# Four column groups instead of two for the last eight rows of wo in a decode layer

## The chip, the cores and the metric

The kernel runs on one core of one Trainium2 chip. The metric is the device time of one execution in microseconds (us), as the median of several runs.

## The reference

One decode step of a layer with two parallel branches, added to the residual x (1 x 1024), all operands bf16:

```
xn  = layernorm(x)
A   = softmax(q k^T / sqrt(128)) v @ wo      # q = xn @ wq: 32 heads of 128, 4 kv heads, last 4096 positions
B   = gelu(layernorm(xn) @ w1 + b1) @ w2 + b2   # w1: 1024 x 3584, w2: 3584 x 1024
out = x + A + B                              # 1 x 1024, wo: 4096 x 1024
```

The keys and values used are 4 x 4096 x 128 each. Together with the four weight matrices some 40 MB are read from memory for one row of output.

## The kernel before

The kernel is written with a tile library: the order of instructions on each engine is the order of the code, save that two places (`tc.issue_after`) tie a few instructions behind a named one, and the library adds the semaphore waits.

All large operands come in on one DMA queue, issued by SyncE in this order: the keys (`kq`), two halves of wq, w1, the values (`v_sb`), w2, and then wo. Each matrix goes into a tile of a small pool; a tile is loaded again when its last reader is done. wo (4096 rows of 1024) is laid out as 32 "rows" of 128 partitions x 1024 columns. Its first 16 rows come in one DMA, the second 16 rows in four: rows 0 to 7, 8 to 12, 13 and 14, and 15 of that half (`cuts` in L218).

The output of both branches is one sum over 60 such rows: 28 of w2, with columns of the hidden vector `hT` as weights, and 32 of wo, with columns of the attention output `o8` as weights. Every row is a contraction over 128 partitions with a single weight column, so the matmul writes one partition. The sum's 1024 columns are two halves of 512; each half has a column group of TensorE and a partition of its own (0 and 32), chosen with `tile_position=(0, 32 * half)`, so that the two halves' matmuls can run side by side. The first 52 rows are summed in the PSUM tile `accf` (L324), which also holds x and b2 from an earlier matmul (L179).

The last 8 rows, those of the last three DMAs, are summed apart (`TAIL = 8`). They go into two PSUM tiles `acct`, which split each half at column `N1 = 280`: `acct[0]` has columns 0 to 279, `acct[1]` columns 280 to 511. Both are first set to zero over 33 partitions by fp32 matmuls with zeros (L322), in the pause after the w2 rows. When `accf` is complete, ScalarE copies its columns 280 to 511 into `bulk[1]` (L328), and VectorE its columns 0 to 279 into `bulk[0]` (L329). Two fp32 matmuls of 33 rows with a column of the identity then bring `bulk[1]` into `acct[1]` (L333). Each tail row is four matmuls (L337): 280 columns for each half, then 232 columns for each half. At the end VectorE adds `acct[0]` and `bulk[0]` into the result row (L341), ScalarE copies `acct[1]` (L342), and two DMAs of one row of 512 values each write the output, one issued by SyncE (L344), one by ScalarE (L345).

At the start GpSimd fills constants: `zb` (with the bf16 identity and the selection matrices), `ones_f`, `mhalf`, `zf` (fp32 zeros and the selection matrix `sel4`) and `gmask`. `ident_f` is the fp32 identity.

Of the kernel before, what the change touches and what calls it, by code (L numbers as in the profile page):

```python
# [7 lines left out]
FP32 = mybir.dt.float32  # L8
BF16 = mybir.dt.bfloat16
ACT = mybir.ActivationFunctionType  # L10
ALU = mybir.AluOpType
# [4 lines left out]
def kernel(  # L16
# [14 lines left out]
    nc = tc.nc  # L31
    P = 128
# [5 lines left out]
    Hq = NQ // Dh  # L38
# [8 lines left out]
    CWO = NQ // P  # L47
# [5 lines left out]
    consts = ctx.enter_context(tc.tile_pool(name="consts", bufs=1))  # L53
# [5 lines left out]
    ps_f = ctx.enter_context(tc.tile_pool(name="ps_f", bufs=2, space=bass.MemoryType.PSUM))  # L59
# [3 lines left out]
    def ring_tile(name):  # L63
        return ring.tile([P, RING_ELEMS], BF16, tag="ring", name=name, align_bytes=256)
# [17 lines left out]
    for i in range(2):  # L82
        t = kq[:, RING_ELEMS:] if i == 0 else ring_tile("wq1")[:]
# [10 lines left out]
                            pattern=[[-1, P]], channel_multiplier=1)  # L94
    ident_f = consts.tile([P, P], FP32)
# [11 lines left out]
    with tc.issue_after(first_exp.ins):  # L107
# [1 line left out]
        nc.scalar.dma_start(out=xb8[0:4, :], in_=x_flat.rearrange("(a n) -> a n", a=4))  # L109
        nc.scalar.dma_start(out=xb8[4:8, :], in_=B_b2.rearrange("(a n) -> a n", a=4))  # L110
        nc.scalar.dma_start(out=b1_8[0:4, :], in_=b1_v[0:4, :])
    zf = consts.tile([P, 512 + Hq], FP32)
    nc.gpsimd.memset(zf[:], 0.0)
    zeros = zf[:, 0:512]
    sel4 = zf[:, 512:]
    qm_f = zb[:, P:P + 160]
    spread = zb[0:Hq, 288:800].rearrange("h (q p) -> h q p", q=4)
    sel_b = zb[0:8, 800:1056].rearrange("k (s m) -> k s m", s=2)
# [1 line left out]
    for sel, base in ((sel_x, 0), (sel_x, -64), (sel_b, 0)):  # L120
        nc.gpsimd.affine_select(out=sel, in_=sel, compare_op=ALU.not_equal, fill=1.0, base=base,
                                pattern=[[-16, 2], [-1, sel.shape[2]]], channel_multiplier=16)
    for R in range(4):
        nc.gpsimd.affine_select(out=sel4, in_=sel4, compare_op=ALU.not_equal, fill=1.0, base=-32 * R,
                                pattern=[[-1, Hq]], channel_multiplier=1)
# [3 lines left out]
                            pattern=[[-1, 4], [1, P]], channel_multiplier=-4)  # L129
# [4 lines left out]
                            pattern=[[-REP, Hkv]], channel_multiplier=1)  # L134
    nc.gpsimd.affine_select(out=gmask[:], in_=gmask[:], compare_op=ALU.is_ge, fill=0.0, base=REP - 1,
                            pattern=[[REP, Hkv]], channel_multiplier=-1)
# [35 lines left out]
    accf = ps_acc.tile([P, 512], FP32, tag="accf")  # L172
# [45 lines left out]
    for i, cuts in enumerate([[0, 16], [0, 8, 13, 15, 16]]):  # L218
        nr = CWO // 2
        t = ring_tile(f"wo{i}")  # L220
# [6 lines left out]
    for i, w3 in enumerate(wq_tiles):  # L227
        for r in range(4):
            c = 4 * i + r
            for j in range(NJQ):  # L230
                b, t = divmod(j, 4)
                nc.tensor.matmul(accq[32 * t:32 * t + 1, b, :], lhsT=xnT[:, c:c + 1], rhs=w3[:, r, j * 512:(j + 1) * 512],  # L232
                                 start=(c == 0), stop=(c == C - 1), tile_position=(0, 32 * t))
# [6 lines left out]
    for c in range(C):  # L240
        for b in range(2):
            for t in range(4):
                j = 2 * t + b
                nc.tensor.matmul(acch[32 * t:32 * t + 1, b, :NH], lhsT=yT[:, c:c + 1], rhs=w1v[:, c, j * NH:(j + 1) * NH],  # L244
                                 start=False, stop=(c == C - 1), tile_position=(0, 32 * t))
# [11 lines left out]
    for a in range(WQ4 // 512):  # L257
        for R in range(4):
            for g in range(Hkv):
                c0 = WQ4 * R + 512 * a  # L260
                nc.tensor.matmul(sp[32 * R:32 * R + 32, a, :], lhsT=qm[:, g, :], rhs=kT[:, g, c0:c0 + 512],  # L261
                                 start=(g == 0), stop=(g == Hkv - 1), tile_position=(0, 32 * R))
# [28 lines left out]
    hT = w2t[:, CW2 * D:CW2 * (D + 32)].rearrange("p (c f) -> p c f", f=32)  # L291
# [4 lines left out]
    for c in range(NCH):  # L296
        nc.tensor.matmul(o_all[:].rearrange("h g d -> h (g d)"), lhsT=eTb[:, 32 * c:32 * c + 32], rhs=v4[:, :, c, :],  # L297
                         start=(c == 0), stop=(c == NCH - 1))
# [6 lines left out]
    o8_ps = ps_f.tile([P, 32], FP32, tag="pf", name="o8_ps")  # L305
    for q in range(4):
        nc.tensor.matmul(o8_ps[:], lhsT=spread[:, q, :], rhs=o_bf[:, 32 * q:32 * q + 32], start=(q == 0), stop=(q == 3))
    o8 = consts.tile([P, 32], BF16)
    nc.scalar.copy(out=o8[:], in_=o8_ps[:])


    vec = {"h": lambda c: hT[:, c, 0:1], "o": lambda c: o8[:, c:c + 1]}
    N1 = 280
    TAIL = 8
    cols = ((0, N1), (N1, 512))
    n_bulk = len(chunk_src) - TAIL
    acct = [ps_f.tile([P, b - a], FP32, tag="pf", name=f"acct{i}") for i, (a, b) in enumerate(cols)]
    for idx, (kind, c, wap) in enumerate(chunk_src[:n_bulk]):
        if idx == CW2:
            with tc.issue_after(last.ins):  # L320
                for t, (a, b) in zip(acct, cols):
                    nc.tensor.matmul(t[0:33, :], lhsT=zeros[:, 0:33], rhs=zeros[:, 0:b - a], start=True, stop=False)  # L322
        for half in range(2):
            last = nc.tensor.matmul(accf[32 * half:32 * half + 1, :], lhsT=vec[kind](c),  # L324
                                    rhs=wap[:, half * 512:(half + 1) * 512],
                                    start=False, stop=(idx == n_bulk - 1), tile_position=(0, 32 * half))
    bulk = [consts.tile([33, b - a], FP32, name=f"bulk{i}") for i, (a, b) in enumerate(cols)]
    nc.scalar.copy(out=bulk[1][:], in_=accf[0:33, N1:512])  # L328
    nc.vector.tensor_copy(out=bulk[0][:], in_=accf[0:33, 0:N1])  # L329
    for idx, (kind, c, wap) in enumerate(chunk_src[n_bulk:]):  # L330
        if idx == 0:
            for half in range(2):
                nc.tensor.matmul(acct[1][32 * half:32 * half + 1, :], lhsT=ident_f[0:33, 32 * half:32 * half + 1], rhs=bulk[1][:],  # L333
                                 start=False, stop=False, tile_position=(0, 32 * half))
        for t, (n0, n1) in zip(acct, cols):
            for half in range(2):
                nc.tensor.matmul(t[32 * half:32 * half + 1, :], lhsT=vec[kind](c),  # L337
                                 rhs=wap[:, half * 512 + n0:half * 512 + n1],
                                 start=False, stop=(idx == TAIL - 1), tile_position=(0, 32 * half))
    res = consts.tile([33, 512], BF16)  # L340
    nc.vector.tensor_tensor(out=res[:, 0:N1], in0=acct[0][0:33, :], in1=bulk[0][:], op=ALU.add)  # L341
    nc.scalar.copy(out=res[:, N1:512], in_=acct[1][0:33, :])  # L342
    out_v = out.rearrange("a b (t n) -> (a b t) n", t=2)
    nc.sync.dma_start(out=out_v[0:1, :], in_=res[0:1, :])  # L344
    nc.scalar.dma_start(out=out_v[1:2, :], in_=res[32:33, :])  # L345


# [28 lines left out]
```

## Time and profile before

| | us |
|---|---|
| median of 3 runs (lowest, highest) | 101.69 (101.53, 101.70) |
| profiled execution: its own time | 101.47 |
| profiled execution: span | 99.8 |
| PE / DVE / ACT / POOL busy | 46.9 / 38.1 / 28.7 / 8.6 |
| DMA, mean over the span | 400 GB/s, 39.91 MB |
| last tail matmuls (L337), first start to last end | 94.96 to 97.18 |
| final VectorE add (L341), start and duration | 97.13, 0.44 |
| final ScalarE copy (L342), start and duration | 97.23, 0.34 |

The span is the part of an execution that the profile shows; the execution's own time is 1.67 us longer. In rows of the profile, L337 is a line of the kernel, PE is TensorE's matmuls, PEld its weight loads, DVE VectorE, ACT ScalarE, POOL GpSimd, SP SyncE. A shape such as 128\*1 128x280 reads: 128 rows and 1 column of weights, 128 partitions x 280 moving columns.

### The profile page before, as it was taken

What the parts mean: (1) busy time and instruction counts of PE and PEld (TensorE: products, weight loads), DVE (VectorE), ACT (ScalarE), POOL (GpSimd) and SP (SyncE); (2) the same over time, 40 slices, a digit from 0 to 9 for tenths busy, and PEclk for the clock granted to TensorE, in tenths of its full rate; (3) what the DMA queues carried; (4) which work ended last, traced back from release to release, by engine and by line L of the source; (5) the groups of instructions that cost most, each with busy time, mean ns of one, the idle gap of its engine ahead of it and who ended that gap; (6) DMA issues with size and microseconds to landing.
All of it is one profiled execution on the core that took longest, in us unless ns stands there. A gap on an engine that the chain in (4) does not pass through costs nothing.

```text
span 99.8 us, 919 instructions
## 1 busy us (share of the span) xinstructions
PE 46.9 (47%) x365; PEld 20.6 (21%) x365; DVE 38.1 (38%) x26; ACT 28.7 (29%) x32; POOL 8.6 (9%) x33
## 2 busy tenths in 40 slices
PE   0005100008400960087259707999200999595880
PEld 0003100002100300053136402334000243241250
DVE  0079999999999960012350024000600000000101
ACT  5306100007999999900240170000010000000101
POOL 7911560000000000000011000000000000000000
PEclk9999999999985588557955795569975599999999
DMA  2899999999999888998499999898899999999920
GB/s 46 374 422 417 440 499 460 473 447 420 420 420 580 368 368 368 391 713 368 200 417 424 430 562 391 368 713 351 368 391 417 420 420 420 407 434 392 395 87 1
DMA packets 2535, 39.91 MB, mean 400 GB/s; under 512 B 338, under 2 KB 356, under 8 KB 612
## 3 DMA queue, kind: packets, MB, share of 16 engines
q1 hardware_dynamic: 2458, 39.85, 93.6%
q8 instruction: 3, 0.05, 0.2%
q10 hardware_dynamic: 74, 0.01, 0.1%
HBM read 39.86 MB, written 0.00 MB: 400 GB/s over the span
## 4 chain that ended last, share of the span: by engine, by line
DMA 79%; PE 16%; SPq 2%; issue 1%; ACT 0%
DMA v_sb<-in_A_v_cache_dram 33%; DMA wo<-in_A_wo_dram 24%; DMA kq<-in_A_wq_dram 17%; PE o_all L297 10%; DMA kq<-in_A_k_cache_dram 5%; PE accq L232 3%; PE acct L337 2%; SPq L209 1%; ACT res L342 0%; SPq L202 0%; SPq L223 0%
## 5 line engine op out<-in xcount | busy, mean ns | idle before, releaser
L195 ACT COPY kt<-kt 32x4096 bf16<-32x4096 bf16 x5 | 18.0, 3601 | 10.4 <-DVE kt L186 10.3
L186 DVE STREAM_TRANSPOSE kt<-kq 128x4096 bf16<-128x4096 bf16 x4 | 17.4, 4414 | 5.7 <-DMA kq<-in_A_k_cache_dram 5.7
L197 DVE COPY kt<-kt 32x4096 bf16<-32x4096 bf16 x11 | 13.4, 1218 | 0.2
L297 PE MATMUL o_all<-v_sb,w1t 128*32 128x512 bf16 x32 | 10.0, 491 | 3.7 <-DMA v_sb<-in_A_v_cache_dram 3.7
L324 PE MATMUL accf<-w2t 128*1 128x512 bf16 x56 | 7.6, 436 | 4.4 <-DMA w2t<-in_B_w_dram 4.4
L329 DVE COPY bulk<-accf 33x280 f32<-33x280 f32 x1 | 0.4, 442 | 21.9 <-ACT bulk L328 21.9
L232 PE MATMUL accq<-kq,xnT 128*1 128x512 bf16 x32 | 3.2, 576 | 10.3 <-DMA kq<-in_A_wq_dram 10.3
L324 PE MATMUL accf<-wo,o 128*1 128x512 bf16 x48 | 5.5, 379 | 2.3 <-DMA wo<-in_A_wo_dram 2.3
L232 PE MATMUL accq<-wq,xnT 128*1 128x512 bf16 x32 | 3.5, 616 | 6.5 <-DMA wq<-in_A_wq_dram 6.5
L232 PEld LDWEIGHTS <-xnT 128*1 128x1 bf16 x64 | 2.0, 115 | 20.7 <-issue 20.6
L328 ACT COPY bulk<-accf 33x232 f32<-33x232 f32 x1 | 0.3, 345 | 20.6 <-PE accf L324 20.6
L244 PE MATMUL acch<-w1t,yT 128*1 128x448 bf16 x64 | 5.8, 551 | 0.0
L297 PEld LDWEIGHTS <-w1t 128*32 128x32 bf16 x32 | 3.8, 121 | 9.9 <-issue 8.0
L324 PEld LDWEIGHTS <-w2t 128*1 128x1 bf16 x56 | 2.7, 93 | 8.9 <-issue 6.4
L292 DVE STREAM_TRANSPOSE w2t<-w1t 128x896 bf16<-128x896 bf16 x1 | 1.7, 1702 | 7.0 <-ACT w1t L289 7.0
L300 DVE TENSOR_TENSOR o_m<-o_all,grs 32x512 f32<-32x512 f32 x1 | 0.7, 679 | 9.7 <-PE o_all L297 9.7
L304 ACT CAST o_bf<-o_f 32x128 bf16<-32x128 f32 x1 | 0.3, 297 | 13.2 <-DVE o_f L302 13.2
L244 PEld LDWEIGHTS <-yT 128*1 128x1 bf16 x64 | 3.6, 121 | 1.8
L140 PE MATMUL x_ps<-x,zb 32*128 32x8 bf16 x4 | 0.2, 162 | 7.8 <-DMA x<-in_A_x_dram 7.8
L248 PE MATMUL qT_ps<-zb,w1t 128*128 128x128 bf16 x8 | 1.0, 310 | 5.7 <-ACT w1t L234 5.7
L288 POOL TENSOR_SCALAR zcol<-l_loc 128x1 f32<-128x1 f32 x1 | 0.2, 238 | 36.2 <-ACT w1t L276 36.2
L261 PE MATMUL sp<-kt,zb 128*32 128x512 bf16 x32 | 3.1, 551 | 0.3 <-DVE zb L253 0.3
(77 smaller groups left out, 40.6 us busy)
## 6 DMA issues: line engine op xcount, KB each, us to landing
w1t<-in_B_w_dram SPq DMA_DIRECT2D x1, 7168.0 KB, 24.7
w2t<-in_B_w_dram SPq DMA_DIRECT2D x1, 7168.0 KB, 30.5
kq<-in_A_k_cache_dram SPq DMA_DIRECT2D x4, 1024.0 KB, 6.9
kq<-in_A_wq_dram SPq DMA_DIRECT2D x1, 4096.0 KB, 17.2
wq<-in_A_wq_dram SPq DMA_DIRECT2D x1, 4096.0 KB, 24.3
v_sb<-in_A_v_cache_dram SPq DMA_DIRECT2D x4, 1024.0 KB, 26.6
wo<-in_A_wo_dram SPq DMA_DIRECT2D x1, 4096.0 KB, 39.8
wo<-in_A_wo_dram SPq DMA_DIRECT2D x1, 2048.0 KB
```

The lines of the kernel that those rows point to most:

```text
L186: nc.vector.transpose(out=scr[:, g, :], in_=k2[:, g, :])
L195: nc.scalar.copy(out=dst, in_=src)
L197: nc.vector.tensor_copy(out=dst, in_=src)
L209: nc.sync.dma_start(out=v4[:, g, :, :], in_=A_v_cache[0, g, Sk - W:Sk, :].rearrange("(p c) d -> p c d", p=P))
L232: nc.tensor.matmul(accq[32 * t:32 * t + 1, b, :], lhsT=xnT[:, c:c + 1], rhs=w3[:, r, j * 512:(j + 1) * 512], start=(c == 0), stop=(c == C ...
L244: nc.tensor.matmul(acch[32 * t:32 * t + 1, b, :NH], lhsT=yT[:, c:c + 1], rhs=w1v[:, c, j * NH:(j + 1) * NH], start=False, stop=(c == C - 1 ...
L248: nc.tensor.transpose(qT_ps[:, b * 4 + hh, :], q_sb[:, b, hh * Dh:(hh + 1) * Dh], ident)
L261: nc.tensor.matmul(sp[32 * R:32 * R + 32, a, :], lhsT=qm[:, g, :], rhs=kT[:, g, c0:c0 + 512], start=(g == 0), stop=(g == Hkv - 1), tile_po ...
L292: nc.vector.transpose(out=hT, in_=h_sb.rearrange("p (d c) -> p c d", c=CW2))
L297: nc.tensor.matmul(o_all[:].rearrange("h g d -> h (g d)"), lhsT=eTb[:, 32 * c:32 * c + 32], rhs=v4[:, :, c, :], start=(c == 0), stop=(c == ...
L324: last = nc.tensor.matmul(accf[32 * half:32 * half + 1, :], lhsT=vec[kind](c), rhs=wap[:, half * 512:(half + 1) * 512], start=False, stop= ...
L337: nc.tensor.matmul(t[32 * half:32 * half + 1, :], lhsT=vec[kind](c), rhs=wap[:, half * 512 + n0:half * 512 + n1], start=False, stop=(idx = ...
```

## The change

The tail is summed in four column groups. Each half of 512 columns is cut in two rows of 256 columns (`r`), and each row in two pieces, of 120 columns (`acct[0]`) and 136 columns (`acct[1]`). `acct[0]` sits on partitions 0 and 1 (half 0) and 32 and 33 (half 1), `acct[1]` on partitions 64 and 65, 96 and 97; partition r of a pair holds row r. So that a matmul adds to one partition of its pair and zero to the other, its weights are two columns: the column of `o8` and a zero, taken from a new tile `o8z` which holds every column between two zero columns. A tail row is now eight matmuls of 120 or 136 columns in place of four of 280 or 232. One ScalarE copy brings all of `accf` into `bulk`. Six fp32 matmuls of 33 rows, in place of two, bring three of the four pieces of each half into `acct`; the fourth (columns 0 to 119 of each half) is still added by VectorE at the end. Their weights are columns of `ident_f` and a new two-column selector `sel01`, made by GpSimd. The final add and copy are 34 x 120 and 34 x 136, and each output DMA writes two rows of 256 values.

```diff
-    zf = consts.tile([P, 512 + Hq], FP32)
+    zf = consts.tile([P, 512 + Hq + 2], FP32)
     nc.gpsimd.memset(zf[:], 0.0)
     zeros = zf[:, 0:512]
-    sel4 = zf[:, 512:]
+    o8z = consts.tile([P, CWO, 3], BF16)
+    nc.gpsimd.memset(o8z[:], 0.0)
+    sel4 = zf[:, 512:512 + Hq]
+    sel01 = zf[0:33, 512 + Hq:]
+    nc.gpsimd.affine_select(out=sel01, in_=sel01, compare_op=ALU.not_equal, fill=1.0, base=-1,
+                            pattern=[[1, 2]], channel_multiplier=2)
...
-    o8 = consts.tile([P, 32], BF16)
-    nc.scalar.copy(out=o8[:], in_=o8_ps[:])
+    nc.scalar.copy(out=o8z[:, :, 1:2], in_=o8_ps[:].unsqueeze(2))
-    vec = {"h": lambda c: hT[:, c, 0:1], "o": lambda c: o8[:, c:c + 1]}
-    N1 = 280
+    vec = {"h": lambda c: hT[:, c, 0:1], "o": lambda c: o8z[:, c, 1:2]}
+    NE = 120
     TAIL = 8
-    cols = ((0, N1), (N1, 512))
+    widths = (NE, 256 - NE)
     n_bulk = len(chunk_src) - TAIL
-    acct = [ps_f.tile([P, b - a], FP32, tag="pf", name=f"acct{i}") for i, (a, b) in enumerate(cols)]
+    acct = [ps_f.tile([P, n], FP32, tag="pf", name=f"acct{i}") for i, n in enumerate(widths)]
     for idx, (kind, c, wap) in enumerate(chunk_src[:n_bulk]):
         if idx == CW2:
             with tc.issue_after(last.ins):
-                for t, (a, b) in zip(acct, cols):
-                    nc.tensor.matmul(t[0:33, :], lhsT=zeros[:, 0:33], rhs=zeros[:, 0:b - a], start=True, stop=False)
+                for i, (t, n) in enumerate(zip(acct, widths)):
+                    nc.tensor.matmul(t[64 * i:64 * i + 34, :], lhsT=zeros[:, 0:34], rhs=zeros[:, 0:n], start=True, stop=False,
+                                     tile_position=(0, 64 * i))
...
-    bulk = [consts.tile([33, b - a], FP32, name=f"bulk{i}") for i, (a, b) in enumerate(cols)]
-    nc.scalar.copy(out=bulk[1][:], in_=accf[0:33, N1:512])
-    nc.vector.tensor_copy(out=bulk[0][:], in_=accf[0:33, 0:N1])
+    bulk = consts.tile([34, 512], FP32, name="bulk")
+    nc.scalar.copy(out=bulk[:], in_=accf[0:34, :])
+    row_sel = {(0, 0): ident_f[0:33, 0:2], (1, 0): ident_f[0:33, 32:34],
+               (0, 1): sel01, (1, 1): ident_f[0:33, 31:33]}
+    parts = [(i, r, half) for r in range(2) for i in range(2) for half in range(2)]
+    cols = ((0, NE), (NE, 256))
     for idx, (kind, c, wap) in enumerate(chunk_src[n_bulk:]):
         if idx == 0:
-            for half in range(2):
-                nc.tensor.matmul(acct[1][32 * half:32 * half + 1, :], lhsT=ident_f[0:33, 32 * half:32 * half + 1], rhs=bulk[1][:],
-                                 start=False, stop=False, tile_position=(0, 32 * half))
-        for t, (n0, n1) in zip(acct, cols):
-            for half in range(2):
-                nc.tensor.matmul(t[32 * half:32 * half + 1, :], lhsT=vec[kind](c),
-                                 rhs=wap[:, half * 512 + n0:half * 512 + n1],
-                                 start=False, stop=(idx == TAIL - 1), tile_position=(0, 32 * half))
-    res = consts.tile([33, 512], BF16)
-    nc.vector.tensor_tensor(out=res[:, 0:N1], in0=acct[0][0:33, :], in1=bulk[0][:], op=ALU.add)
-    nc.scalar.copy(out=res[:, N1:512], in_=acct[1][0:33, :])
-    out_v = out.rearrange("a b (t n) -> (a b t) n", t=2)
-    nc.sync.dma_start(out=out_v[0:1, :], in_=res[0:1, :])
-    nc.scalar.dma_start(out=out_v[1:2, :], in_=res[32:33, :])
+            for i, r, half in [(1, 0, 0), (1, 0, 1), (0, 1, 0), (0, 1, 1), (1, 1, 0), (1, 1, 1)]:
+                g0 = 64 * i + 32 * half
+                nc.tensor.matmul(acct[i][g0:g0 + 2, :], lhsT=row_sel[(half, r)],
+                                 rhs=bulk[0:33, 256 * r + cols[i][0]:256 * r + cols[i][1]],
+                                 start=False, stop=False, tile_position=(0, g0))
+        for i, r, half in parts:
+            g0 = 64 * i + 32 * half
+            w0 = 512 * half + 256 * r
+            nc.tensor.matmul(acct[i][g0:g0 + 2, :], lhsT=o8z[:, c, 1 - r:3 - r], rhs=wap[:, w0 + cols[i][0]:w0 + cols[i][1]],
+                             start=False, stop=(idx == TAIL - 1 and r == 1), tile_position=(0, g0))
+    res = consts.tile([34, 256], BF16)
+    nc.vector.tensor_tensor(out=res[:, 0:NE], in0=acct[0][0:34, :], in1=bulk[:, 0:NE], op=ALU.add)
+    nc.scalar.copy(out=res[:, NE:256], in_=acct[1][64:98, :])
+    out_v = out.rearrange("a b (t n) -> (a b t) n", t=4)
+    nc.sync.dma_start(out=out_v[0:2, :], in_=res[0:2, :])
+    nc.scalar.dma_start(out=out_v[2:4, :], in_=res[32:34, :])
```

## The prediction

> **What bounds the kernel now.** I read the page's chain shares first, then the chain in order of time.
>
> ```profile
> DMA 79%; PE 16%; SPq 2%; issue 1%; ACT 0%
> ```
>
> ```profile
> 70.95 23.97 DMA wo<-in_A_wo_dram
> 94.92 0.04 issue
> 94.96 1.82 PE acct L337 x28
> 96.78 0.02 issue
> 96.80 0.40 PE acct L337 x4
> 97.20 0.02 issue
> 97.23 0.34 ACT res L342
> ```
>
> The kernel is a DMA stream with a short end behind it. In the chain 28 tail matmuls look like 1.82 us of TensorE work, and the change halves the columns per group. But the DMA list (KB and us from issue to landing) and the windows (length, busy time of PE, PEld, DVE, ACT, POOL, granted clock, DMA share, GB/s) say otherwise:
>
> ```profile
> wo<-in_A_wo_dram SPq DMA_DIRECT2D x1, 1280.0 KB, 24.0
> wo<-in_A_wo_dram SPq DMA_DIRECT2D x1, 512.0 KB, 24.7
> ...
> 94.00:94.90 0.90, 0.56 (x4) 0.17 (x5) 0.44 (x1) 0.19 (x1) 0.00 (x0) 1.00 1.02 405
> 94.90:95.70 0.80, 0.74 (x14) 0.60 (x15) 0.00 (x0) 0.00 (x0) 0.00 (x0) 1.00 0.36 138
> 95.70:96.45 0.75, 0.75 (x16) 0.49 (x14) 0.00 (x0) 0.00 (x0) 0.00 (x0) 1.00 0.12 44
> ```
>
> The 512 KB DMA (rows 13 and 14) was issued at 71.43, so it landed at 96.13; from 95.70 to 96.45 a share of 0.12, two engines of 16, still moves data. The trace's landing records give the tail's three DMAs as complete at 94.92, 96.14 and 96.76. Single matmul starts fit: five rows start at 94.964, two at 96.179, the last at 96.801, each 0.04 us after a landing. Inside a burst a row starts every 0.218 us, so before the second landing TensorE stands 0.13 us (94.964 + 5 x 0.218 = 96.05), before the third 0.19. Only what follows 96.80 is on the path: one row, the final add and copy, the output DMAs.
>
> ```profile
> 93.85 0.34 ACT L328 COPY bulk<-accf 33x232 f32<-33x232 f32 x1 [20.63 <-PE accf L324]
> 94.22 0.44 DVE L329 COPY bulk<-accf 33x280 f32<-33x280 f32 x1 [21.86 <-ACT bulk L328]
> ...
> 94.25 0.56 PE L333 MATMUL acct<-bulk,ident_f 33*1 33x232 f32 x4 [0.44 <-ACT bulk L328]
> ...
> 97.13 0.44 DVE L341 TENSOR_TENSOR res<-acct,bulk 33x280 bf16<-33x280 f32 x1 [2.46 <-PE acct L337]
> 97.23 0.34 ACT L342 CAST res<-acct 33x232 bf16<-33x232 f32 x1 [3.03 <-PE acct L337]
> 97.65 0.25 ACTq L345 DMA_DIRECT2D out_dram<-res  x1
> 97.65 0.26 SPq L344 DMA_DIRECT2D out_dram<-res  x1
> ```
>
> VectorE and ScalarE end together at 97.57, and both output DMAs go 0.08 us later.
>
> **Constants.** GpSimd gets a memset of `o8z` and one select more, some 0.1 and 0.2 us by the memsets (0.09 to 0.20) and selects (0.18 to 0.21) of its start. They stand ahead of the selections for x_ps (weights ready at 4.53) and of `zf` for ScalarE's zeroing copy (4.09). The x_ps matmul waits for x until 7.82, so 3 us cover them; bare, they would cost 0.3. Writing `o8z` with a stride keeps a copy of 32 columns (0.185 us at 73.0), behind which only w2 rows queue that wait for a landing at 77.37. The zeroing matmuls shrink, inside the pause from 85.9 to 87.07. SyncE's loads keep order and place. All these I take at nothing.
>
> **The bulk.** The two copies become one of 512 columns. ScalarE took 345 ns for 232 columns and 1012 for 1024, 0.842 ns a column: 345 + 280 x 0.842 = 581 ns. It ends at 93.85 + 0.58 = 94.43, 0.24 later than L328 did, and the fp32 matmuls queued behind it start at 94.48. In L333 the passes start at 94.246, 94.252, 94.441 and 94.447: each matmul makes two passes, a pass of 232 columns takes 0.195, the two groups run together. A pass of 136 is then 0.114, of 120 0.101. Three pairs one after another: 2 x (0.114 + 0.101 + 0.114) = 0.66, to 95.14. All four groups at once: 4 x 0.114, to 94.94. Nothing together: 8 x 0.114 + 4 x 0.101 = 1.32, to 95.80. I take 95.14, since L333 shows pairs. That is 0.18 after the first landing, but before TensorE's next forced wait.
>
> **Seven rows under cover.** They must be through by 96.80, so with a start at 95.14 a row may take up to 0.237 us. Starts of pairs follow each other in L337 by 118 ns at 280 columns and 99 at 232: 0.42 ns a column and 1 or 2 ns. Four groups at once are seen in L232 (window 22.84 to 22.90):
>
> ```profile
> 22.85 0.60 PE L232 MATMUL accq<-kq,xnT 128*1 128x512 bf16 x4 [10.26 <-DMA kq<-in_A_wq_dram]
> ```
>
> Its four matmuls start at 22.850, 22.853, 22.857 and 22.860, and later ones keep that spacing every 427 ns, at half clock; the tail's windows grant 1.00. So a set of four here takes some 58 ns (136 columns), a row 0.116, seven 0.81: 95.95. Even at today's 0.218 they end at 96.67. All of it costs and gains nothing.
>
> **Behind the last landing.** Matmuls last 279 ns for 280 columns and 261 for 232, so about 164 + 0.417 a column: 214 for 120, 220 for 136. The last row's first set starts at 96.801 to 96.81, the second at 96.854 (120 columns, both halves by 96.857) and 96.87. VectorE's piece is written at 97.07, ScalarE's at 97.09; both start 0.042 later, as now: 97.11 and 97.13. VectorE took 443 ns for 280 columns and 679 for 512, 1.02 a column: 278 for 120, end 97.39. ScalarE: 345 - 96 x 0.842 = 264 for 136, end 97.40. Now: 97.57. Gain 0.17: a little from TensorE, most from narrower final operations.
>
> **Output.** Each DMA writes two rows of 512 B instead of one of 1024 B. Issues in the trace take 0.25 for one row (L345) and 0.25 for four (L110); a 1024 B packet takes 44 ns. Bounds: 0.02 gained, if two shorter packets move together, to 0.10 lost, if a second packet and its completion queue behind the first. I take nothing, as L110 has the nearer count.
>
> Sum: 101.47 - 0.17 = 101.30 for the profiled execution, which lies 0.22 under the median. For the median: 101.69 - 0.17 = **101.52**. This measurement can tell about 0.2%, or 0.2 us, from no change, so the gain stands just under what shows.
>
> **Rivals.** (1) *A floor per matmul.* Eight matmuls of 53 ns replace four of 110. In the x_ps group matmuls of 8 columns start at 7.824, 7.849, 7.877 and 7.904, 25 to 28 ns apart, with a weight load each:
>
> ```profile
> 7.82 0.24 PE L140 MATMUL x_ps<-x,zb 32*128 32x8 bf16 x4 [7.82 <-DMA x<-in_A_x_dram]
> ```
>
> At 25 ns each a row takes 0.2, still covered; but in the last row VectorE's last matmul starts at 96.93 and ScalarE's at 96.98: ends 97.46 and 97.50, gain 0.07, 101.62. Against it: L140 uses the whole array's columns, L232 four groups 3 ns apart. The Trainium skill (TensorEngine Tiling, Instruction Overhead) has the rule that speaks against this change: a matmul has some 60 cycles of overhead, and a small dimension should not be cut further. L140's spacing agrees, L232's doesn't. Chance 0.13.
>
> (2) *Slower: weight loads come into the open.* In L337 a load takes 79 to 84 ns, less than the 99 between pairs, and lies inside them. A set of 58 ns cannot hide it. If matmuls must wait for the end of their load, sets follow at 58 + 84 = 142, a row takes 0.284, over the 0.237 that decides; seven rows end at 97.13, VectorE starts at 97.53 and ends at 97.81: 0.24 slower, 101.93. Against it: in L140 a matmul starts 23 ns after the start of a load of 99. Chance 0.09.
>
> (3) *The four groups do not run side by side* (the change doesn't do what it says): a row takes 4 x 51 + 4 x 58 = 436 ns, the last one starts at 98.19, ScalarE ends near 99.1: 1.5 slower, 103.2. L232 speaks against it. Chance 0.03.
>
> (4) *An instruction fetch meets the last row.* The page's instruction queue has three packets; the trace starts them at 48.80, 69.16 and 96.56, each of 16 KB and 0.92 to 0.94 us. From 50 on one of the 16 engines lands 1.2 us late on every load, from 75 on two. The third starts after the data. TensorE's stream grows by 80 instructions (32 more matmuls with their loads, four more fp32 matmuls of two passes and two loads each), and its same place is now reached up to 0.45 earlier, with the fp32 matmuls; on one of the late engines a fetch at 96.1 would hold the last row by 0.93: 102.45. On another it finds its engine idle since 95.64. The Trainium skill (Runtime: NRT & Kernel Launch, Instruction fetch mechanics) says that blocks of 16 KiB, 256 instructions, are fetched by the sequencer's own DMA queue; packet size and queue agree. Two late engines in 16, and no fetch yet on the same one twice: chance 0.07.
>
> **How the numbers follow.** Forecast 0.62, rivals 0.13, 0.09, 0.03, 0.07, other causes 0.06. Around the forecast's 0.17 lie the output's -0.02 to 0.10 and the runs' spread of 0.17 from lowest to highest: I give 0.29 to more than 0.2 us and 0.33 to less. Faster 0.29 + 0.01 = 0.30; within 0.33 + 0.13 + 0.01 = 0.47; slower 0.09 + 0.03 + 0.07 + 0.04 = 0.23. Low end: 0.17, 0.02 with the best output, and half the spread, 0.09: 101.41, taken as 101.40. High end 101.95, which takes in rivals 1 and 2; outside remain 3 and 4 and some of the rest, 0.14. The forecast's own range is 101.40 to 101.71 (0.10 lost at the output, half the spread).
>
> **What would show it.** Right: last-row matmuls still start at about 96.80, in sets 50 to 60 ns apart; VectorE near 0.28 and ScalarE near 0.26, both starting about 0.31 us after that row; the fp32 passes end by 95.2. Wrong: starts 25 ns apart, or sets 90 or more (rivals 1, 2); a landing later than 96.8, or a fetch packet before it; output packets that end more than 0.9 us after their issue (now 0.8).

## The result, and the profile after

Each kernel was executed 22 times on the same chip.

| | before | after |
|---|---|---|
| median, lowest to highest, us | 101.60 (101.06 to 101.92) | 101.86 (101.61 to 102.09) |
| after to before | | 1.0031, 95% interval 1.002 to 1.0041 |
| profiled execution: own time | 101.47 | 101.61 |
| profiled execution: span | 99.76 | 99.49 |
| own time less span | 1.71 | 2.12 |

The forecast was 0.17 us less; the kernel became 0.26 us slower, by its medians, a small loss that lies clear of noise. The last two rows are the finding: what the profile shows got shorter, what it does not show got longer. That is no accident of the profiled execution: over its 22 executions the changed kernel's own time is 2.12 us above its span (median; 2.05 to 2.23). For the kernel before, in the executions run beside the experiments below, the same difference has a median of 1.72 to 1.74 (1.67 to 1.89). The two ranges do not meet. It is called the **outside time** here.

The chain shares of the page after, with a little less PE in them than before (16%):

```profile
DMA 79%; PE 14%; SPq 3%; issue 1%; DVE 0%; DVEq 0%
```

The end of the chain in order of time (start, length, what it was):

```profile
71.41 25.20 DMA wo<-in_A_wo_dram
96.61 0.04 issue
96.65 0.33 PE acct L348 x8
96.98 0.01 DVEq L351
96.99 0.04 issue
97.03 0.28 DVE res L351
```

The 28 tail matmuls that stood in the chain of before are gone; only the eight of the last row are left, behind the last landing at 96.61. That is the prediction's reading: the rest of TensorE's tail work was never on the path. The windows (length, busy time of PE, PEld, DVE, ACT, POOL, granted clock, DMA share, GB/s) say the same, since TensorE now stands idle for half of the second stretch:

```profile
94.75:95.55 0.80, 0.80 (x44) 0.57 (x41) 0.00 (x0) 0.00 (x0) 0.00 (x0) 1.00 0.44 172
95.55:96.30 0.75, 0.37 (x22) 0.24 (x16) 0.00 (x0) 0.00 (x0) 0.00 (x0) 1.00 0.20 66
```

The timeline of the tail (start, length, engine, line, operation, count, idle time before it and what ended that):

```profile
93.70 0.58 ACT L333 COPY bulk<-accf 34x512 f32<-34x512 f32 x1 [20.95 <-PE accf L329]
94.34 0.28 PE L342 MATMUL acct<-bulk,ident_f 33*2 33x136 f32 x2 [0.67 <-ACT bulk L333]
...
94.89 0.76 PE L348 MATMUL acct<-wo,o8z 128*2 128x120 bf16 x40
...
96.65 0.29 PE L348 MATMUL acct<-wo,o8z 128*2 128x120 bf16 x8 [0.20 <-DMA wo<-in_A_wo_dram]
97.00 0.27 ACT L352 CAST res<-acct 34x136 bf16<-34x136 f32 x1 [2.72 <-PE acct L348]
97.03 0.28 DVE L351 TENSOR_TENSOR res<-acct,bulk 34x120 bf16<-34x120 f32 x1 [25.15 <-PE acct L348]
97.38 0.26 ACTq L355 DMA_DIRECT2D out_dram<-res  x1
97.39 0.27 SPq L354 DMA_DIRECT2D out_dram<-res  x1
```

Landings move by some tenths of a us from one execution to the next (the last one lay between 96.6 and 97.2 in the profiles of this study), so the end is best measured from the last landing:

| us after the last landing | before | after | experiment e12 (below) |
|---|---|---|---|
| VectorE's add starts | 0.368 | 0.423 | 0.352 |
| VectorE's add ends | 0.811 | 0.698 | 0.627 |
| ScalarE's copy ends | 0.812 | 0.664 | 0.663 |
| SyncE's output DMA issued | 0.892 | 0.779 | 0.710 |
| its data landed | 2.168 | 2.054 | 1.990 |
| span ends | 2.998 | 2.884 | 2.820 |

The change gains 0.114 us there. In all three kernels SyncE issues its DMA 0.08 us after VectorE's add ends, also in e12, where ScalarE's copy ends after the add; by these figures it is the add that sets the end. So two questions stand: what put 0.40 us outside the span, and why the end gained 0.11 in place of 0.17.

### The profile page after: what moved, and what is told of

Same layout as the page of the kernel before. It is cut to its first block, busy times and chain, and to the rows that moved or that the text cites. A ratio compares the mean times of both kernels' runs of the same rounds, so it can differ in the third digit from the quotient of the medians.

```text
span 99.5 us, 1001 instructions
## 1 busy us (share of the span) xinstructions
PE 47.6 (48%) x405; PEld 20.2 (20%) x405; DVE 37.5 (38%) x25; ACT 28.9 (29%) x32; POOL 8.9 (9%) x35
## 4 chain that ended last, share of the span: by engine, by line
DMA 79%; PE 14%; SPq 3%; issue 1%; DVE 0%; DVEq 0%
DMA v_sb<-in_A_v_cache_dram 32%; DMA wo<-in_A_wo_dram 25%; DMA kq<-in_A_wq_dram 17%; PE o_all L302 10%; DMA kq<-in_A_k_cache_dram 5%; PE accq L237 4%; SPq L214 1%; SPq L228 1%; SPq L207 0%; PE acct L348 0%; DVE res L351 0%; DVEq L351 0%
## 5 line engine op out<-in xcount | busy, mean ns | idle before, releaser
L329 PE MATMUL accf<-w2t 128*1 128x512 bf16 x56 | 8.9, 496 | 4.8 <-DMA w2t<-in_B_w_dram 4.8
L333 ACT COPY bulk<-accf 34x512 f32<-34x512 f32 x1 | 0.6, 579 | 20.9 <-PE accf L329 20.9
L329 PE MATMUL accf<-wo,o8z 128*1 128x512 bf16 x48 | 5.5, 379 | 1.6 <-DMA wo<-in_A_wo_dram 1.6
L249 PE MATMUL acch<-w1t,yT 128*1 128x448 bf16 x64 | 5.1, 488 | 0.0
L266 PE MATMUL sp<-kt,zb 128*32 128x512 bf16 x32 | 3.7, 631 | 0.3 <-DVE zb L258 0.3
L249 PEld LDWEIGHTS <-yT 128*1 128x1 bf16 x64 | 3.1, 108 | 1.5
```

## The experiments

Sixteen kernels. Every ratio is against the kernel before, executed beside it on the same chip. "Outside" is own time less span, a median. Three things in the change could reach past the last traced instruction: TensorE's longer stream of instructions (823 in place of 743), the outputs in two rows each, and the constants that GpSimd makes (its stream, counted in the built programs with its register, branch and semaphore instructions, goes from 58 to 61).

**e1_pad80.** The kernel before, with TensorE's stream at the changed kernel's length, behind the zero matmuls of L322:

```diff
+            for _ in range(20):
+                nc.tensor.matmul(acct[0][0:1, 0:8], lhsT=zeros[:, 0:1], rhs=zeros[:, 0:8], start=False, stop=False)
```

> The kernel before with 20 fp32 matmuls of zeros (8 columns, 1 weight column) in the pause behind L322: 80 more TensorE instructions, as many as the change adds (743 to 823), none of them ahead of a landing on the path. Stream theory (what lies outside the span grows with TensorE's instruction count): span as before, 99.8 to 100.0, own time less span 2.1 instead of 1.7, time 0.4 us (0.4%) over before. Output theory and constants theory: own time less span 1.7, time within 0.1% of before.

101.55 against 101.50 us, ratio 1.0003 (0.9995 to 1.0012), outside 1.72. TensorE's 80 instructions cost nothing.

**e2_pad20.** The same with `range(5)`, TensorE's stream at 763.

> As the run with 80 more TensorE instructions, but with 5 such matmuls, 20 instructions (763). Stream theory in proportion to the count (0.43 us for 80): own time less span 1.8, time 0.1% over before. Stream theory with a step at a boundary: either 1.7 and no change, or 2.1 and 0.4% slower. Output and constants theories: 1.7 and no change.

101.61 us, 1.0009 (0.9999 to 1.002), outside 1.76. Nothing again.

**e3_after_less80.** The changed kernel without the matmuls of the first 20 rows of w2, so that TensorE's stream is 743 long as before:

```diff
     for idx, (kind, c, wap) in enumerate(chunk_src[:n_bulk]):
+        if idx < 20:
+            continue
```

> The changed kernel without the matmuls of the first 20 rows of w2 (40 matmuls with their loads; that part of the sum is left out, the data is still loaded): TensorE has 743 instructions again. Stream theory: own time less span back at 1.7, span as after (99.7), time 0.2 us (0.2%) under before. Output and constants theories: own time less span stays 2.1, time as after, 0.3% over before.

101.90 us, 1.0054 (1.0028 to 1.0079), outside 2.11 (one of its eight executions had 3.29). The loss stays without the longer stream. With e1, TensorE's stream is out.

**e4_two_piece_out.** The kernel before, split at column 256, each output DMA reading two pieces of 512 B with a gap between them from one partition:

```diff
-    N1 = 280
+    N1 = 256
...
+    out_v = out.rearrange("a b (h t n) -> (a b h) t n", h=2, t=2)
+    nc.sync.dma_start(out=out_v[0:1, :, :], in_=res[0:1, :, 0:N1])
+    nc.scalar.dma_start(out=out_v[1:2, :, :], in_=res[32:33, :, 0:N1])
```

> The kernel before with each output DMA writing two pieces of 512 B (result tile with a gap, split at column 256 instead of 280). Output theory: own time less span 2.1, time 0.4% over before. Stream and constants theories: own time less span 1.7; the split costs 0.02 us on ScalarE, so time within 0.1% of before.

102.12 us, 1.0064 (1.0052 to 1.0076), but outside 1.72: the whole loss is in the span, 100.4 us, where no theory had expected one. Behind the last landing the span ends 0.65 us later than before, and most of that, 0.44 us, is in the issue of the two DMAs, which the timeline shows at 0.71 and 0.67 where a plain row takes 0.26 and 0.25:

```profile
97.58 0.71 SPq L344 DMA_DIRECT2D out_dram<-res  x1
97.59 0.67 ACTq L345 DMA_DIRECT2D out_dram<-res  x1
```

The changed kernel's issues take 0.27 and 0.26. So this form is dear, but it is not the change's form, and it adds nothing outside.

**e5_consts_only.** The kernel before with GpSimd's new lines alone; nothing reads what they make:

```diff
-    zf = consts.tile([P, 512 + Hq], FP32)
+    zf = consts.tile([P, 512 + Hq + 2], FP32)
...
+    o8z = consts.tile([P, CWO, 3], BF16)
+    nc.gpsimd.memset(o8z[:], 0.0)
...
+    nc.gpsimd.affine_select(out=sel01, in_=sel01, compare_op=ALU.not_equal, fill=1.0, base=-1,
+                            pattern=[[1, 2]], channel_multiplier=2)
```

> The kernel before with GpSimd's part of the change alone: the memset of o8z, the selector sel01 and the two columns more in zf, not used by anything. Constants theory (more GpSimd work at the start lengthens what lies outside the span): own time less span 2.1 instead of 1.7, span as before (99.8), time 0.4% over before. Output theory (output DMAs that write two rows from two partitions do it): 1.7, time within 0.1% of before.

102.21 against 101.74 us, 1.0048 (1.0021 to 1.0074), outside 2.16. The tail, the outputs and TensorE are those of before, and the loss is there.

**e6_consts_off_pool.** The changed kernel with the same constants made by other engines:

```diff
-    nc.gpsimd.memset(o8z[:], 0.0)
...
-    nc.gpsimd.affine_select(out=sel01, in_=sel01, compare_op=ALU.not_equal, fill=1.0, base=-1,
-                            pattern=[[1, 2]], channel_multiplier=2)
+    nc.vector.memset(o8z[:], 0.0)
...
+    sel01_t = consts.tile([33, 2], FP32)
+    nc.scalar.copy(out=sel01_t[:, 0:1], in_=ident_f[0:33, 64:65])
+    nc.scalar.copy(out=sel01_t[:, 1:2], in_=ident_f[0:33, 0:1])
```

> The changed kernel with o8z cleared by VectorE and sel01 copied from the identity by ScalarE, so GpSimd has as many instructions as before. Constants theory: own time less span back at 1.7, span 99.6 to 99.7 as after, time 0.1 to 0.2% under before. Output theory: 2.1, time as after, 0.3% over before.

101.47 against 101.74 us, 0.9991 (0.9968 to 1.0014), outside 1.76. e5 and e6 are the pair that decides: GpSimd's three instructions bring the 0.4 us, and without them it is gone. Inside the span no cost of them shows: in e5's trace the span ends 3.0 us after the last landing, as before, and in e6's 2.886 us after it, as in the changed kernel (2.884).

**e7_one_out_dma.** The kernel before with one output DMA, issued by SyncE, for both rows (partitions 0 and 32):

```diff
-    nc.sync.dma_start(out=out_v[0:1, :], in_=res[0:1, :])
-    nc.scalar.dma_start(out=out_v[1:2, :], in_=res[32:33, :])
+    nc.sync.dma_start(out=out_v[0:2, :], in_=res[0:33:32, :])
```

> The kernel before with one output DMA, issued by SyncE, that writes both rows of 512 values from partitions 0 and 32. Output theory: own time less span 2.1; the span itself about as before (one issue of some 0.27 us instead of two side by side). Constants theory: 1.7, time within 0.1% of before.

102.09 us, 1.0034 (1.0007 to 1.0061), outside 1.77. The issue takes 0.58 us, and the span ends 3.40 after the last landing, 0.41 later than before, though it was expected to stay about the same. Again a cost inside the span, and none outside.

**e8_four_out_dmas.** The changed kernel with four output DMAs of one row:

```diff
-    nc.sync.dma_start(out=out_v[0:2, :], in_=res[0:2, :])
-    nc.scalar.dma_start(out=out_v[2:4, :], in_=res[32:34, :])
+    for i, row in enumerate((0, 1, 32, 33)):
+        (nc.sync if i < 2 else nc.scalar).dma_start(out=out_v[i:i + 1, :], in_=res[row:row + 1, :])
```

> The changed kernel with four output DMAs of one row of 256 values each, two issued by SyncE and two by ScalarE. Output theory: own time less span 1.7; the span 0.25 longer than after (a second issue on each queue), 99.9 to 100.0, time within 0.1% of before. Constants theory: 2.1, time 0.25 us over after, 0.55% over before.

102.40 us, 1.007 (1.0043 to 1.0098), outside 2.14: the span ends 3.39 us after the last landing, 0.51 later than in the changed kernel (0.25 was expected), some 0.3 of it the second issue on each queue. The outside time stays where GpSimd's 61 instructions put it. With e6, which has the changed kernel's output DMAs and 1.76 outside, the outputs are out as a cause.

**e9_memset_only, e10_select_only, e11_three_memsets.** The kernel before with the memset of `o8z` alone (GpSimd's stream 59), with the select alone (60), and with three memsets of one column into tiles that nothing reads (61). They tell the operation from the count; the edit of e11 is:

```diff
+    for i in range(3):
+        pad = consts.tile([P, 1], FP32, name=f"pad{i}")
+        nc.gpsimd.memset(pad[:], 0.0)
```

> The kernel before with the memset of o8z alone (GpSimd 59 instructions instead of 58). Kind theory (what the added GpSimd instructions do lengthens the time outside the span): either this run or the one with the select alone shows own time less span at 2.1, the other 1.7. Count theory with a step (GpSimd's instruction count passes a boundary): 1.7 here if the boundary lies at 60 or 61, 2.1 if at 59. Count in proportion (0.4 us for 3 instructions): 1.85.

> The kernel before with the selector alone (two columns more in zf, its select and the register move that goes with it: 60 instructions). Kind theory: 2.1 if the select is the kind that counts, else 1.7. Count theory with a step: 2.1 if the boundary lies at 59 or 60, 1.7 if at 61. In proportion: 2.0.

> The kernel before with three GpSimd memsets of one column each, used by nothing (61 instructions, as in the changed kernel, but neither its tile nor a select). Count theory, step or in proportion: own time less span 2.1, time 0.4% over before. Kind theory with the select: 1.7, time as before; with memsets of any size: 2.1, and then the run with one memset shows it too.

Against 101.64 us: 59 gives 101.61, 1.0012 (0.9993 to 1.003), outside 1.70; 60 gives 101.80, 1.0018 (1.0002 to 1.0035), outside 1.98; 61 gives 102.05, 1.0049 (1.0032 to 1.0066), outside 2.11. Three small memsets cost as much as the change's constants, and one big memset costs nothing: the count matters, and not what is done. No theory had all three: a cost in proportion gives the 1.98 at 60, but not the 1.70 at 59 (it had 1.85), and a single step gives no value between 1.7 and 2.1.

**e12_split_bulk.** The changed kernel with e6's constants, and with VectorE bringing over its own 120 columns behind ScalarE's copy, so that the last add waits for TensorE alone:

```diff
+    bulk0 = consts.tile([34, NE], FP32, name="bulk0")
-    nc.scalar.copy(out=bulk[:], in_=accf[0:34, :])
+    nc.scalar.copy(out=bulk[:, NE:512], in_=accf[0:34, NE:512])
+    nc.vector.tensor_copy(out=bulk0[:], in_=accf[0:34, 0:NE])
...
-    nc.vector.tensor_tensor(out=res[:, 0:NE], in0=acct[0][0:34, :], in1=bulk[:, 0:NE], op=ALU.add)
+    nc.vector.tensor_tensor(out=res[:, 0:NE], in0=acct[0][0:34, :], in1=bulk0[:], op=ALU.add)
```

> The changed kernel with its constants made by VectorE and ScalarE as in the run without them on GpSimd, and with accf's first 120 columns of each half copied by VectorE itself after ScalarE's copy of the other 392, so that the last add waits for TensorE alone. Theory that the change gains behind the last landing and loses outside the span: own time less span 1.7, the last add starts 0.03 to 0.05 us earlier after the last landing than in the changed kernel, time 0.2% under before and 0.5% under the changed kernel. Rival (the change has no gain of its own): time within 0.1% of before.

101.45 against 101.64 us, 0.998 (0.9964 to 0.9996), outside 1.73. It is 0.2% faster than the kernel before, and so, by the ratio of each to that kernel, 0.5% faster than the changed one, which did not run beside it. Its timeline has VectorE ahead of ScalarE, 0.31 behind the last row's first matmul, and both outputs issued together:

```profile
96.97 0.29 PE L351 MATMUL acct<-wo,o8z 128*2 128x120 bf16 x8 [0.23 <-DMA wo<-in_A_wo_dram]
...
97.28 0.28 DVE L354 TENSOR_TENSOR res<-acct,bulk 34x120 bf16<-34x120 f32 x1 [2.49 <-PE acct L351]
97.33 0.27 ACT L355 CAST res<-acct 34x136 bf16<-34x136 f32 x1 [2.84 <-PE acct L351]
97.64 0.26 ACTq L358 DMA_DIRECT2D out_dram<-res  x1
97.64 0.27 SPq L357 DMA_DIRECT2D out_dram<-res  x1
```

In e6, with the same constants and ScalarE's single copy, the add starts 0.38 behind that matmul and 0.03 after ScalarE, as in the changed kernel:

```profile
96.99 0.29 PE L349 MATMUL acct<-wo,o8z 128*2 128x120 bf16 x8 [0.23 <-DMA wo<-in_A_wo_dram]
...
97.34 0.27 ACT L353 CAST res<-acct 34x136 bf16<-34x136 f32 x1 [2.86 <-PE acct L349]
97.37 0.28 DVE L352 TENSOR_TENSOR res<-acct,bulk 34x120 bf16<-34x120 f32 x1 [26.13 <-PE acct L349]
```

From the last landing e12 gains 2.998 - 2.820 = 0.178 us on the kernel before; the forecast had 0.17. The forecast's number was right for a kernel with that one wait. The add starts 0.07 us earlier than in the changed kernel, where 0.03 to 0.05 was expected.

**e13_six_memsets, e14_eighteen_memsets.** e11 with 6 memsets, and with 18 into a single tile (GpSimd's stream 64 and 76), to see whether the cost grows with the count or belongs to a place in the stream.

> The kernel before with six GpSimd memsets of one column each (64 instructions). Step theory (a boundary between 59 and 61, then a fixed cost): own time less span 2.1 to 2.2. Growth theory (some 0.13 us for each instruction over 59 or 60): 2.5. Span as before.

> The kernel before with 18 such memsets (76 instructions). Step theory: own time less span 2.1 to 2.2, time 0.4% over before. Growth theory: 4.0, time 2.2% over before. Span as before: 18 memsets of some 0.05 us still end before x lands at 7.8.

Against 101.73 us: 64 gives 101.87, 1.0019 (0.9988 to 1.0051), outside 1.87; 76 gives 101.67, 0.9999 (0.9976 to 1.0023), outside 1.71. Neither the step (2.1 to 2.2 for both) nor the growth (2.5 and 4.0) came out: the cost is there at 60, smaller at 64, and gone at 76. The median of e13 hides two kinds of execution: seven of its ten have an outside time of 1.83 to 1.90, three of 2.24 to 2.42.

The traces have packets of instructions on two queues, q8 and q14. On q14 every trace, that of the kernel before too, has six or seven packets of 8 KB between 11.5 and 7.7 us ahead of the span. e13, e14 and later e16 have one more, behind the span's start, and no other trace has. In e13 a window from 95 to 103 us, which goes past the span's end at 99.9, has it among the DMA queues (packets, MB, share of 16 engines), beside TensorE's packet on q8:

```profile
q8 instruction: 1, 0.02, 1.0%
q14 instruction: 1, 0.01, 0.4%
```

The packet, of 8 KB, starts at 102.11, 2.2 us behind the span's end, and takes 0.47 us; the own time of that execution was 102.28, 2.38 more than its span, so that it is one of the three long ones. In e14 the window from 56 to 59 us has it, in the middle of the stream of weights:

```profile
q14 instruction: 1, 0.01, 0.6%
```

There it starts at 57.30. With twelve more GpSimd instructions the packet lies well inside the kernel, and no longer behind it.

**e15_three_late.** The kernel before with three more GpSimd operations behind the one for `zcol`, some 50 us in (stream 61), to tell an early delay from the count:

```diff
+    for i in range(3):
+        pad = consts.tile([P, 1], FP32, name=f"pad{i}")
+        nc.gpsimd.tensor_scalar_mul(out=pad[:], in0=zcol[:], scalar1=0.0)
```

> The kernel before with three GpSimd multiplies of one column each behind zcol, some 50 us into the kernel (61 instructions). Count theory: own time less span 2.1, as with three early memsets, time 0.4% over before. Early-work theory (what counts is GpSimd's work at the start): 1.7, time as before.

102.11 against 101.73 us, 1.0042 (1.0019 to 1.0065), outside 2.10. Whether the three stand at the start or 50 us in does not matter.

**e16_after_padded.** The changed kernel as it is, with 15 more one-column memsets on GpSimd (stream 76). If a place in the stream costs the 0.4 us, more work must take it away.

> The changed kernel, all of it, with 15 more GpSimd memsets of one column each (76 instructions instead of 61). Boundary theory (a block of GpSimd's instructions is fetched in the open at the end of the execution with 60 to 64 instructions, and under the kernel with 76): own time less span 1.7, an 8 KB packet of instructions in the middle of the kernel, span 99.7 as after, time 0.4% under the changed kernel and 0.1 to 0.2% under before, with more work. Count theory as it was (more instructions cost more): 2.1 or more, time at least 0.3% over before.

101.60 against 101.57 us, 1.0001 (0.9984 to 1.0017), outside 1.74 in place of 2.12, and q14's packet at 56.79. The outside time went as expected. That the kernel would then lie under the one before did not show: its span of 99.85 (median) was no shorter than that of before here, 99.80. In its trace the span ends 2.907 us after the last landing, so the gain at the end is there, but 0.1 us is less than this comparison can tell (its interval is 0.16% to either side).

All of it by the length of GpSimd's stream:

| instructions of GpSimd | kernels | outside, us |
|---|---|---|
| 58 | before, e1, e2, e4, e6, e7, e12 | 1.72 to 1.77 |
| 59 | e9 | 1.70 |
| 60 | e10 | 1.98 |
| 61 | after, e3, e5, e8, e11, e15 | 2.10 to 2.16 |
| 64 | e13 | 1.87 |
| 76 | e14, e16 | 1.71, 1.74 |

## Why the prediction went wrong, step by step

**Constants: the step that failed.** The prediction costed the `o8z` memset and the select by their durations and the 3 us that cover them, and took them "at nothing". Their durations are near the estimates of 0.1 and 0.2 us (start, length):

```profile
2.82 0.17 POOL L116 MEMSET o8z<- 128x96 bf16 x1
...
3.20 0.18 POOL L119 TENSOR_SCALAR_AFFINE_SELECT zf<-zf 33x2 f32<-33x2 f32 x1
```

Nothing waits for them in the span. But they count as instructions of GpSimd, and by that count the execution got 0.40 us longer outside the span. The prediction counted TensorE's stream with care (rival 4) and not GpSimd's.

**The last line of the sum failed with it.** "101.47 - 0.17", and the same 0.17 off the median, holds only if what lies outside the span is the same for both kernels. The page of before gave that part as 1.67 us (1.71 by the finer span) and nothing in it said that it was fixed. By the runs: 0.40 more outside, 0.11 less behind the last landing, so 0.29 slower; measured 0.26 by the medians and 0.31% by the ratio. That 101.86 lies inside the stated range of 101.40 to 101.95 is luck: the range reached so far up for rivals 1 and 2, and neither happened.

**What is shown of the cause, and what is not.** Shown: the outside time depends on how many instructions GpSimd's stream has, not on which (e5, e11, e15) nor on TensorE's stream or the outputs (e1 to e4, e6 to e8). Of the lengths that ran, 60, 61 and 64 add 0.13 to 0.43 us to that of the kernel before in the same round, and 59 and 76 add nothing. With the stream at 64 a packet on q14 lies behind the span, with 76 inside it.

Not shown: how the count makes the time. The reading offered here is that the stream crosses a block's boundary at the very end of an execution when it has 60 to 64 instructions, and that the execution waits for that block. For 60 and 61 no trace holds a packet on q14 in the span or behind it, and why 64 mostly costs less than 61 is open. The one packet that was caught speaks against a wait for all of it: it ends 2.68 us behind the span's end, and the own time of that execution is only 2.38 longer than its span. Own time less span also does not tell whether the added time lies behind the span or ahead of it. The Trainium skill (Runtime: NRT & Kernel Launch, Instruction fetch mechanics) says that instructions come in 16 KiB blocks on the sequencer's own queue and that crossing a boundary is mostly hidden. TensorE's packets here are 16 KB and harmless: 80 more instructions in e1 moved the third from 96.56 to 91.16 us at no cost. The packet on q14 that comes with a longer GpSimd stream is 8 KB, and at 76 it costs nothing either; no run shows that a crossing is what costs at 60 to 64.

**Start of VectorE's last add: mis-sized.** Forecast 0.31 us behind the last row's first matmul; measured 0.38, and the add ended last, 0.034 behind ScalarE's copy. It now waits for two engines: for TensorE, and for ScalarE, whose copy writes the part of `bulk` that it adds; that copy ended at 94.28, long before. In the trace a semaphore instruction of VectorE, which waits for TensorE, stands at 96.965, ahead of the add at 97.031; the kernel before and e12 have none there. Before, VectorE had copied its part itself. e12 gives it that back and starts 0.07 earlier, which brings the gain from 0.114 to 0.178. The prediction merged the two copies and priced the copy, but not the wait that it adds.

**What was right.** Only the last landing matters, and the savings in the seven other rows bring nothing. The last row starts 0.04 after its landing. In the two column groups of 120 columns a matmul follows every 52 ns, in the two of 136 every 58 to 59 ns, forecast 53 and 58, and all four run at once; a row takes 0.118 us, forecast 0.116. ScalarE's bulk copy took 0.579 us (0.581), the add 0.275 (0.278), the last copy 0.269 (0.264; it started 0.02 later than forecast, at no cost). The output DMAs of two rows took 0.255 and 0.273 us to issue and landed 1.275 us after the issue, against 1.276 before, so that "nothing" was right for them. The fp32 passes took 0.115 us (0.114), and all four groups overlapped in part, so that they were done at 94.80, not 95.14; under cover in either case. One reading is not borne out by the granted clock: the prediction put L232's 427 ns down to half clock, but the profile grants 1.00 there (22.84 to 26.00 us) as in the tail; why its 512 columns take 0.83 ns a column in place of 0.42 no run here shows. The forecast used its spacing of 3 to 4 ns alone, which the tail has too.

**The rivals.** A floor of 25 ns per matmul, weight loads in the open (142 ns a set), and groups that don't run side by side: all three are refuted by matmuls that follow each other every 52 to 59 ns in each of four column groups at once. The Trainium skill (TensorEngine Tiling (Array Packing), Instruction Overhead) gives each matmul some 60 cycles of overhead. As a floor for one matmul after another, which is how rival 1 has it (25 ns from L140), that makes, by estimate, 100 ns between sets of four, and the trace disagrees for matmuls in column groups. The instruction fetch of TensorE came earlier, as rival 4 had it (95.90 in place of 96.56), and held no landing. Its idea, that a boundary in a stream of instructions may cost, could be the right one on another engine, at another place; that is not shown.

## What to carry to other kernels

Make two subtractions on each result, the span's and the own time less span: a loss in the second is not in any row of the profile, and no work on the rows will find it. Count the instructions that a change adds on every engine's stream, the idle one's too; where own time less span jumps, add or take away a few idle instructions on one engine at a time; here e1, e6 and e11 showed in that way which engine it was. And when two producers of an operand become one, look at which engine the last consumer now waits for: a wait for a result that is long done still cost 0.07 us here.

## What the runs showed of the hardware

- GpSimd's stream with 60, 61 or 64 instructions made an execution 0.13 to 0.43 us longer, all of it outside the span; with 59 or 76 it was as long as with 58. The instruction packet that came with the longer streams has 8 KB, where TensorE's have 16 KB.
- The issue of an output DMA depends on its form more than on its size: one row, 0.25 to 0.26 us; two rows from neighbouring partitions, 0.26 to 0.27; one DMA over partitions 0 and 32, 0.58; two pieces with a gap from one partition, 0.67 to 0.71.
- Four column groups of 120 or 136 columns, each with its own weight loads, run at once; in each a matmul starts every 52 to 59 ns.
- An add of VectorE that waits for TensorE and for a copy of ScalarE that is long done started 0.07 us later than one that waits for TensorE alone (0.423 and 0.352 us after the last landing).
